# An adaLN attention block on one core: scale rows and K steps in another order, 1/sigma turned later, and a last tile in other widths

## The chip, the cores and the metric

The kernel runs on one NeuronCore of a Trainium2 chip. Its engines work side by side, each through its own list of instructions in order: TensorE (PE; its weight loads are shown apart as PEld), VectorE (DVE), ScalarE (ACT), GpSimd (POOL), and SyncE (SP), which here only issues DMA transfers. The metric is the device time of one execution in microseconds (us). The kernel before takes 99.05 us, the median of three runs (98.73 to 99.12).

## The reference

Inputs are x (2, 256, 1152), c (2, 1152), wqkv (1152, 3456), wo (1152, 1152) and w_mod (1152, 6912), all bf16. Of the six rows of modulation only shift_a, scale_a and gate_a are used.

```
mod = (silu(c) @ w_mod).reshape(B, 6, 1, D)
shift_a, scale_a, gate_a, ... = mod[:, i]
h   = layernorm(x) * (1 + scale_a) + shift_a          # eps 1e-5
qkv = h @ wqkv ; q, k, v = split(qkv)
p   = softmax(q @ k.T * D ** -0.5)                    # one head of 1152
a   = (p @ v) @ wo
return x + gate_a * a
```

## The kernel before

There are 512 tokens in four tiles of 128 (tiles 0 and 1 are batch 0, tiles 2 and 3 are batch 1), and D = 1152 is nine blocks of 128, called k here. Nearly all of the work is matmuls on PE; the order of every engine's instructions is pinned to the order in which the code emits them (`pin`, at the end), so an instruction that waits holds up all that stands behind it on its engine. A helper records the instructions, which is why the profile shows one line, L74, for almost all.

**Loads.** SP issues the loads in one queue: x tiles 1, 0 and 3; the scale rows of w_mod for the first 384 columns (wS, in five loads); K's weights of block 0 (wK, its first 1024 columns), of block 1; x tile 2; block 2; and then, by thirds of the columns, more of wS and wK, the shift rows (wH), the weights of Q and V (wqv), the gate rows (wG) and wo (wO). Eight transfers may be under way; each further issue waits for the load eight places ahead of it.

**Front.** PE runs 13 filler matmuls on a constant tile (`fillers`, junk_rhs). Meanwhile ACT and DVE form the silu of c (`silu_c`, whose last step copies it 27 times side by side into scT_rep), the token means (`dve_stats` and `dve_aggr` for tile 1, `act_mean` for the others) and the centred rows xc (`centre`). PE turns xc block by block (`turned`, into PSUM tiles tp), and DVE or ACT copies the turned blocks to xnT (`from_psum`). The variance is needed later only: `act_var`, or the statistics of DVE for tiles 1 and 3.

**Scale rows.** `scale_A(kk)` multiplies one of nine slices of wS with scT_rep, for three blocks of columns, and sums over kk into PSUM (psS0 and psSA). What comes out is 1 + scale for k = 0, 1, 2 (s1p). `scale_part` does the same for k = 3 to 5 (psM) and k = 6 to 8 (psL). DVE scales xnT by it (`scaled`), which gives hTs, the input of K without shift and without 1/sigma.

**K.** Six column blocks of K are summed in six PSUM tiles (accs), one step for each k: `k_part(k, tokens)` for k = 0 to 2 in pieces of the tokens as tiles become ready, `k_step(k)` for all 512 tokens and k = 3 to 8. Two more column blocks (`early_half`, psE) are summed for k = 0 to 2 and finished afterwards by `k_block`. K can leave out 1/sigma, because the scores are multiplied by it later (rstd_bc), and the shift, because it adds the same to all scores of a query.

**1/sigma.** POOL raises the four variances to the power of minus one half and splits each number in three bf16 parts (`rstd_parts`). `rstd_turn` turns the parts on PE (DVE copies them to parts_t), `rstd_spread` spreads them over all partitions with four matmuls (ACT copies them to rstd_bc). Nine DVE multiplications then put 1/sigma into xnT, which Q and V need.

**After K.** `shift_block` forms the shift rows (psH, sh), `modulated` the full h (hT). Q, the scores, V, the softmax and p @ v follow. DVE sums the gate rows beside them (gacc), and POOL reduces them over the partitions.

**Output.** The last loop makes the four tiles of tokens of the output in chunks of columns: nine matmuls each, then DVE multiplies by the gate and adds x. For the last 192 columns of the last tile the gate is in the weights already (wo_last) and x is added by a matmul with the identity, so a plain copy by ACT is enough (`pregated`). PSUM tiles come from three pools: six with the tag mm, and one each with the tags pa and pb; a new tile of a tag waits until the old one's readers are done.

Of the kernel before, what the change touches and what calls it, by code (L numbers as in the profile page):

```python
# [10 lines left out]
F32 = mybir.dt.float32  # L11
# [5 lines left out]
def kernel(  # L17
# [78 lines left out]
    def tok(b):  # L96
        return slice(b * N, (b + 1) * N)
# [4 lines left out]
        out=ident, in_=ident, compare_op=ALU.not_equal, fill=1.0, base=0,  # L102
        pattern=[[-1, P]], channel_multiplier=1,
    )
    junk_rhs = const.tile([P, 512], BF16)
    vec.memset(junk_rhs, 1.0)
    ones_bf = const.tile([P, P], BF16)
    gps.memset(ones_bf, 1.0)
# [36 lines left out]
    def load_k(k0, k1, c0=0, c1=D):  # L145
        spq.dma_start(out=wK[:, k0:k1, c0:c1], in_=wqkv_v[:, k0:k1, D + c0 : D + c1])
# [5 lines left out]
    load_x(3)  # L152
    for k0, k1 in PAIRS:
        load_mod(wS, 1, k0, k1, 0, CA)
    load_k(0, 1, 0, WE)
    load_k(1, 2, 0, WE)
    load_x(2)
    load_k(2, 3, 0, WE)
# [12 lines left out]


    cT = c_sb.rearrange("p b k -> p (b k)")
    junk_ps = psum.tile([P, 512], F32, tag="mm")

    def fillers(n):
        for _ in range(n):
            ten.matmul(junk_ps, lhsT=junk_rhs[:, 0:P], rhs=junk_rhs, start=True, stop=True)

    fillers(13)  # L180
    e_sb = small.tile([P, 2 * KT], F32, tag="e_sb")
# [4 lines left out]
    def silu_c():  # L186
        vec.tensor_scalar_add(out=e_sb, in0=e_sb, scalar1=1.0)
        vec.reciprocal(out=e_sb, in_=e_sb)
        vec.tensor_tensor(
            out=scT_f.rearrange("p k b -> p b k"),  # L190
            in0=c_sb,
            in1=e_sb.rearrange("p (b k) -> p b k", b=B),
            op=ALU.mult,
        )
        sca.copy(out=scT_rep, in_=scT_f.unsqueeze(2).to_broadcast([P, KT, NR // B, B]))

    def sc_rhs(kk):
# [13 lines left out]
    def dve_stats(t, s):  # L211
        vec.bn_stats(out=stats[t][:, s, :], in_=x_sb[:, t, s * CW : (s + 1) * CW])
# [8 lines left out]
    def act_mean(t):  # L221
        sca.activation(out=xc[:, t, :], in_=x_sb[:, t, :], func=ACT.Copy, accum_out=sums[:, t, 0:1])
        sca.activation(out=mv[:, t, 0:1], in_=sums[:, t, 0:1], func=ACT.Copy, scale=1.0 / D)
# [6 lines left out]
    def centre(t, c0=0, c1=D):  # L230
        vec.tensor_scalar(out=xc[:, t, c0:c1], in0=x_sb[:, t, c0:c1], scalar1=mv[:, t, 0:1], scalar2=None,
                          op0=ALU.subtract)
# [8 lines left out]
    def from_psum(eng, t, k0, k1, tp, j0=0):  # L241
        dst, srct = xnT[:, k0:k1, t * P : (t + 1) * P], tp[:, j0 : j0 + k1 - k0, :]
        if eng is vec:
            vec.tensor_copy(out=dst, in_=srct)
        else:
            sca.copy(out=dst, in_=srct)
# [41 lines left out]
    def scale_A(kk):  # L288
        for j in range(KA):
            ten.matmul(  # L290
                psS0 if j == 0 else psSA[:, j - 1, :], lhsT=wS[:, kk, j * P : (j + 1) * P], rhs=sc_rhs(kk),
                start=False, stop=(kk == KT - 1), skip_group_check=True,
            )
# [22 lines left out]
    def one(t):  # L316
        return slice(t * P, (t + 1) * P)
# [4 lines left out]
    def k_part(k, sl, first=False):  # L322
        for f in range(NACC):
            ten.matmul(
                accs[f][:, sl], lhsT=wK[:, k, f * P : (f + 1) * P], rhs=hTs[:, k, sl],
                start=first, stop=False, skip_group_check=True,
            )
# [32 lines left out]
    centre(1)  # L360
    act_mean(0)
    centre(0)
    act_mean(3)

    def bank(name="tp", n=KT - KA, pool=psum, tag="mm"):
# [4 lines left out]
    turned(tp1b, tiles_of(1, KA, KT))  # L370
    from_psum(vec, 1, 0, KA, tp1a)
    from_psum(vec, 1, KA, KT, tp1b)
    scale_A(0)
    scale_A(1)
    fillers(1)
    turned(tp0a, tiles_of(0, 0, KA))
    turned(tp0b, tiles_of(0, KA, KT))
    from_psum(vec, 0, 0, KA, tp0a)
    from_psum(sca, 0, KA, KT, tp0b)
    for kk in range(2, KT):  # L380
        scale_A(kk)
    act_var(0)

# [16 lines left out]
    for k in range(KA):  # L400
        scaled(k, one(3), s1p[:, k, 1:2])
    from_psum(sca, 3, KA, KT - 1, tp3, KA)
    k_part(2, tok(0))
    k_part(0, one(3))
    k_part(1, one(3))
    dve_stats(3, 1)
    centre(2)
    act_var(2)
    tp2 = bank(n=KT - 1, pool=psum_b, tag="pb")
    turned(tp2, tiles_of(2, 0, KT - 1))  # L410
    from_psum(vec, 2, 0, KA, tp2)
    for k in range(KA):
        scaled(k, one(2), s1p[:, k, 1:2])
    k_part(2, one(3))
    early_half(1, 0, psE)
    early_half(2, 0, psE)
    sca.copy(out=early[:, :, tok(0)], in_=psE)
    from_psum(sca, 2, KA, KT - 1, tp2, KA)
    dve_stats(3, 2)
    dve_aggr(3)  # L420
    var_eps(1)
    var_eps(3)
    rstd_parts()
    for k in range(KA - 1):
        k_part(k, one(2))
    psM = psum_a.tile([P, KA, NR], F32, tag="pa")
    for kk in range(KT):
        scale_part(psM, KA, kk)
    scaled_part(psM, KA)
    k_part(KA - 1, one(2))  # L430
    psE = psum_b.tile([P, NEARLY, N], F32, tag="pb")
    for k in range(KA):
        early_half(k, 1, psE)
# [7 lines left out]
    from_psum(vec, 3, KT - 1, KT, tp8, 0)  # L441
    from_psum(vec, 2, KT - 1, KT, tp8, 1)
    k_step(KA + 1)
    rstd_turn()
    k_step(KA + 2, 0, 1)
    rstd_spread()
    psL = psum_b.tile([P, KA, NR], F32, tag="pb")
    for kk in range(KT):
        scale_part(psL, KM, kk)
    scaled_part(psL, KM)  # L450
    k_step(KA + 2, 1, NACC)
    for k in range(KT):
        vec.tensor_tensor(out=xnT[:, k, :], in0=xnT[:, k, :], in1=rstd_bc, op=ALU.mult)
    for k in range(KM, KT):
        k_step(k)
    for f in range(NACC):
        evac(1, qkT[:, KT + f, :], accs[f])
# [154 lines left out]
        pT_sbs.append(pT)  # L612
    for gidx in range(TT * NCH):
        v_group(gidx)
    LASTW = 64
    TAILW = CW // 2
    wo_last = const.tile([P, KT, TAILW], BF16)

# [21 lines left out]
    for t in range(TT):  # L640
        b = t // NQ
        o_sb = work.tile([P, D], BF16, tag="o_sb")
        if t < TT - 1:
            chunks = [(oc * CW, CW) for oc in range(NCH)]
            dma_after = {NCH - 1: (0, D)}
        else:
            chunks = [(0, CW), (CW, CW), (2 * CW, CW - TAILW), (D - TAILW, TAILW - LASTW), (D - LASTW, LASTW)]
            dma_after = {1: (0, 2 * CW), 2: (2 * CW, CW - TAILW), 4: (D - TAILW, TAILW)}
        for ci, (c0, w_) in enumerate(chunks):
            cs = slice(c0, c0 + w_)  # L650
            last = (t == TT - 1) and (ci == len(chunks) - 1)
            pregated = (t == TT - 1) and c0 >= D - TAILW
            ps = psum.tile([P, w_], F32, tag="mm")
            if pregated:
                ten.matmul(ps, lhsT=ident, rhs=x_sb[:, t, cs], start=True, stop=False)
            for k in range(KT):
                ten.matmul(
                    ps, lhsT=attnT[:, k, t * P : (t + 1) * P],
                    rhs=(wo_last[:, k, c0 - (D - TAILW) : c0 - (D - TAILW) + w_] if pregated else wO[:, k, cs]),
                    start=(k == 0 and not pregated), stop=(k == KT - 1),  # L660
                )
            if pregated:
                sca.copy(out=o_sb[:, cs], in_=ps)
            else:
                ga = work.tile([P, CW], F32, tag="ga")
                vec.tensor_tensor(out=ga[:, :w_], in0=ps, in1=gate_bc[:, b, cs], op=ALU.mult)
                vec.tensor_tensor(out=o_sb[:, cs], in0=ga[:, :w_], in1=x_sb[:, t, cs], op=ALU.add)
            if t == NQ - 1:
                gated_columns(vec, 2 * ci, 2 * ci + 2)
            if ci in dma_after:  # L670
                d0, dw = dma_after[ci]
                dma_eng = nc.scalar if last else spq
                dma_eng.dma_start(out=out_f[t * P : (t + 1) * P, d0 : d0 + dw], in_=o_sb[:, d0 : d0 + dw])
# [36 lines left out]
```

## Time and profile before

| what | value |
|---|---|
| median of three runs | 99.05 us |
| the profiled execution | 98.6 us |
| its span, first to last instruction | 96.8 us |
| PE busy | 91.3 us (94%) |
| DVE busy | 70.7 us (73%) |
| ACT busy | 33.9 us (35%) |
| POOL busy | 22.1 us (23%) |
| moved by DMA | 21.31 MB, 220 GB/s over the span |

Rows of a timeline give the start in us from the span's first instruction, the time of one or of several instructions from first start to last end, the engine, the line, the operation, what it writes and reads, the shape, the count, and in brackets how long the engine stood idle before and what ended that. Matmuls overlap: one of 128 columns is shown with 0.22 us, though the next begins 0.056 us later, so the distance between starts is what a matmul costs. The list of waits gives the time waited in total, how many times, and the longest. A row of the stretches view gives the stretch, its length, busy time and count of each engine, then the granted clock of PE, the busy share of the DMA engines and GB/s.

### The profile page before, as it was taken

The page shows a single profiled execution, that of the slowest core. Times are in us where ns is not written, and L with a number is a line of the kernel's source. Part 1 is how long each engine was busy: PE and PEld are TensorE (multiplying, and loading weights), DVE is VectorE, ACT ScalarE, POOL GpSimd, SP SyncE. Part 2 cuts the span into 40 slices and gives each one's busy share as a digit, 9 for nine tenths or more (in the row PEclk, how much of TensorE's full clock was granted, in tenths as well). Part 3 has the DMA queues.
Part 4 walks back from the last instruction along what each step waited for, and adds up shares of the span by engine and source line. Part 5 has one row for each costly group of instructions (what it writes and reads, how often), then busy time and mean ns, then how long its engine had stood idle before and what let it go on. Part 6 is the DMA issues. An engine that isn't in the chain of part 4 may idle for free.

```text
span 96.8 us, 1825 instructions
## 1 busy us (share of the span) xinstructions
PE 91.3 (94%) x726; PEld 55.8 (58%) x731; DVE 70.7 (73%) x138; ACT 33.9 (35%) x68; POOL 22.1 (23%) x26
## 2 busy tenths in 40 slices
PE   3998989999999999999999999999999999999970
PEld 1347969554476444444448766556668765566570
DVE  2468677509985999999992999991228577998870
ACT  5189875220380972242222436332115400000010
POOL 6600005600000000000000000007999980035000
PEclk9999999999999999999999999999999999999999
DMA  2999999999999999999999501110000000303203
GB/s 80 285 340 344 321 383 374 396 388 405 402 375 403 381 413 386 375 370 365 378 401 409 218 6 43 40 26 0 0 0 0 7 0 0 122 0 122 96 31 116
DMA packets 18871, 21.31 MB, mean 220 GB/s; under 512 B 2864, under 2 KB 13360, under 8 KB 18864
## 3 DMA queue, kind: packets, MB, share of 16 engines
q1 hardware_dynamic: 18448, 21.16, 61.2%
q10 hardware_dynamic: 416, 0.05, 0.3%
q8 instruction: 5, 0.08, 0.3%
q14 instruction: 2, 0.02, 0.0%
HBM read 19.76 MB, written 1.18 MB: 216 GB/s over the span
## 4 chain that ended last, share of the span: by engine, by line
PE 91%; DVE 4%; issue 1%
PE ps L74 61%; PE acc L74 11%; PE junk_ps L74 6%; PE s_ps L74 4%; PE tp L74 2%; PE psH L74 2%; PE psE L74 1%; DVE o_sb L74 1%; DVE ga L74 1%; PE psL L74 1%; DVE hTs L74 1%; PE psM L74 1%; PE psSA L74 1%; DVE junk_rhs L74 1%; DVE stats L74 0%
## 5 line engine op out<-in xcount | busy, mean ns | idle before, releaser
L74 POOL PARTITION_ALL_REDUCE gate_bc<-gacc x2 | 13.7, 6887 | 47.0 <-DVE gacc L74 47.0
L74 DVE SCALAR_TENSOR_TENSOR gacc<-wG,scT_f,gacc 128x1152 f32<-128x1152 bf16 x16 | 22.7, 1417 | 0.5
L74 PE MATMUL ps<-wqv,hT 128*128 128x384 bf16 x108 | 17.7, 326 | 0.0
L74 PE MATMUL ps<-hT,wqv 128*128 128x512 bf16 x80 | 17.6, 379 | 0.1
L74 PE MATMUL ps<-wO,attnT 128*128 128x384 bf16 (+1 forms) x108 | 17.0, 319 | 0.0
L74 PEld LDWEIGHTS <-attnT 128*128 128x128 bf16 x126 | 11.3, 98 | 6.4
L74 PEld LDWEIGHTS <-hT 128*128 128x128 bf16 x108 | 10.6, 98 | 6.9
L74 PE MATMUL acc<-hTs,wK 128*128 128x128 bf16 (+2 forms) x88 | 13.4, 292 | 0.5 <-DVE s1p L74 0.4
L74 PEld LDWEIGHTS <-wK 128*128 128x128 bf16 x123 | 10.0, 97 | 6.5 <-DMA wK<-in_wqkv_dram 0.5
L74 PEld LDWEIGHTS <-wqv 128*128 128x128 bf16 x81 | 7.9, 98 | 9.6 <-DVE hT L74 0.4
L74 ACT CAST qkT<-ps 128x512 bf16<-128x512 f32 x10 | 5.8, 584 | 10.9 <-PE ps L74 10.9
L74 DVE TENSOR_TENSOR ga<-ps,gate_bc 128x384 f32<-128x384 f32 (+1 forms) x12 | 6.4, 537 | 2.8 <-PE ps L74 2.8
L74 ACT CAST v_sb<-ps 128x384 bf16<-128x384 f32 x10 | 4.7, 476 | 9.8 <-PE ps L74 9.8
L74 PE MATMUL junk_ps<-junk_rhs 128*128 128x512 bf16 x14 | 5.7, 580 | 1.5 <-DVE junk_rhs L74 1.5
L74 DVE TENSOR_TENSOR o_sb<-ga,x_sb 128x384 bf16<-128x384 f32 (+1 forms) x12 | 6.8, 565 | 0.4
L74 ACT CAST o_sb<-ps 128x128 bf16<-128x128 f32 (+1 forms) x2 | 0.5, 240 | 17.0 <-PE ps L74 17.0
L74 DVE TENSOR_TENSOR xnT<-xnT,rstd_bc 128x512 bf16<-128x512 bf16 x9 | 5.5, 683 | 0.0
L74 PE MATMUL ps<-hTs,wK 128*128 128x512 bf16 x19 | 4.9, 378 | 0.1
L74 DVE CAST attnT<-ps 128x512 bf16<-128x512 f32 (+1 forms) x6 | 3.5, 602 | 1.7 <-PE ps L74 1.7
L74 DVE BATCH_NORM_STATS2 stats<-x_sb 128x6 f32<-128x384 bf16 x6 | 3.2, 553 | 2.1 <-DMA x_sb<-in_x_dram 2.1
L74 PEld LDWEIGHTS <-junk_rhs 128*128 128x128 bf16 x14 | 1.9, 140 | 4.5 <-issue 3.0
L74 ACT CAST qkT<-acc 128x512 bf16<-128x512 f32 x6 | 3.0, 611 | 4.1 <-PE acc L74 4.1
(83 smaller groups left out, 91.4 us busy)
## 6 DMA issues: line engine op xcount, KB each, us to landing
wqv<-in_wqkv_dram SPq DMA_DIRECT2D x5, 864.0 KB, 10.1
wG<-in_w_mod_dram SPq DMA_DIRECT2D x3, 864.0 KB, 10.1
wO<-in_wo_dram SPq DMA_DIRECT2D x3, 864.0 KB, 8.8
wH<-in_w_mod_dram SPq DMA_DIRECT2D x4, 576.0 KB, 7.6
wS<-in_w_mod_dram SPq DMA_DIRECT2D x6, 288.0 KB, 6.4
wK<-in_wqkv_dram SPq DMA_DIRECT2D x6, 288.0 KB, 6.7
x_sb<-in_x_dram SPq DMA_DIRECT2D x4, 288.0 KB, 4.3
wqv<-in_wqkv_dram SPq DMA_DIRECT2D x3, 288.0 KB, 9.0
```

The costliest lines, as they stand in the source:

```text
L74: r = fn(*a, **k)
```

## The change

- The fillers' constant tile is 128 columns wide; the matmul reads it four times over (a repeated axis).
- K's first load, 1024 columns of block 0, is issued as two, of 384 and 640 columns.
- The copy to scT_rep is a function of its own (`silu_rep`) and stands on ACT behind the first `act_mean`.
- Four instead of two slices of the scale rows come between the turning of tile 1 and of tile 0, and the filler there is gone.
- The early columns for k = 1 and 2 of batch 0 stand around `k_part(2, tok(0))`. All of tile 3's `k_part` come before tile 2 is turned, all of tile 2's after psM. Tile 2 is centred ahead of the second statistics step of tile 3, and its variance is squared after the copy of its turned blocks.
- psL follows two of the six matmuls of k = 5; `rstd_turn` follows k = 5, and `rstd_spread` follows k = 6.
- The last tile has chunks of 384, 288, 288 and 192 columns instead of 384, 384, 192, 128 and 64. The last chunk is copied by ACT (128 columns) and DVE (64). In the program as built, that DVE copy waits for ACT's semaphore, and the last store waits for DVE's.

```diff
-    junk_rhs = const.tile([P, 512], BF16)
+    junk_rhs = const.tile([P, P], BF16)
...
-    load_k(0, 1, 0, WE)
+    load_k(0, 1, 0, CA)
+    load_k(0, 1, CA, WE)
...
-    junk_ps = psum.tile([P, 512], F32, tag="mm")
+    junk_ps = psum.tile([P, 4, P], F32, tag="mm")
...
-            ten.matmul(junk_ps, lhsT=junk_rhs[:, 0:P], rhs=junk_rhs, start=True, stop=True)
+            ten.matmul(junk_ps, lhsT=junk_rhs, rhs=junk_rhs.unsqueeze(1).to_broadcast([P, 4, P]),
+                       start=True, stop=True)
...
+
+    def silu_rep():
         sca.copy(out=scT_rep, in_=scT_f.unsqueeze(2).to_broadcast([P, KT, NR // B, B]))
...
     centre(0)
+    silu_rep()
     act_mean(3)
...
-    scale_A(0)
-    scale_A(1)
-    fillers(1)
+    for kk in range(4):
+        scale_A(kk)
     turned(tp0a, tiles_of(0, 0, KA))
...
-    for kk in range(2, KT):
+    for kk in range(4, KT):
         scale_A(kk)
...
+    early_half(1, 0, psE)
     k_part(2, tok(0))
-    k_part(0, one(3))
-    k_part(1, one(3))
+    early_half(2, 0, psE)
+    sca.copy(out=early[:, :, tok(0)], in_=psE)
+    for k in range(KA):
+        k_part(k, one(3))
+    centre(2)
     dve_stats(3, 1)
-    centre(2)
-    act_var(2)
+    dve_stats(3, 2)
     tp2 = bank(n=KT - 1, pool=psum_b, tag="pb")
     turned(tp2, tiles_of(2, 0, KT - 1))
     from_psum(vec, 2, 0, KA, tp2)
     for k in range(KA):
         scaled(k, one(2), s1p[:, k, 1:2])
-    k_part(2, one(3))
-    early_half(1, 0, psE)
-    early_half(2, 0, psE)
-    sca.copy(out=early[:, :, tok(0)], in_=psE)
+    dve_aggr(3)
     from_psum(sca, 2, KA, KT - 1, tp2, KA)
-    dve_stats(3, 2)
-    dve_aggr(3)
+    act_var(2)
     var_eps(1)
     var_eps(3)
     rstd_parts()
-    for k in range(KA - 1):
-        k_part(k, one(2))
...
     scaled_part(psM, KA)
-    k_part(KA - 1, one(2))
+    for k in range(KA):
+        k_part(k, one(2))
...
     k_step(KA + 1)
-    rstd_turn()
-    k_step(KA + 2, 0, 1)
-    rstd_spread()
+    k_step(KA + 2, 0, 2)
...
     scaled_part(psL, KM)
-    k_step(KA + 2, 1, NACC)
+    k_step(KA + 2, 2, NACC)
+    rstd_turn()
+    k_step(KM)
+    rstd_spread()
     for k in range(KT):
         vec.tensor_tensor(out=xnT[:, k, :], in0=xnT[:, k, :], in1=rstd_bc, op=ALU.mult)
-    for k in range(KM, KT):
+    for k in range(KM + 1, KT):
         k_step(k)
...
-            chunks = [(0, CW), (CW, CW), (2 * CW, CW - TAILW), (D - TAILW, TAILW - LASTW), (D - LASTW, LASTW)]
-            dma_after = {1: (0, 2 * CW), 2: (2 * CW, CW - TAILW), 4: (D - TAILW, TAILW)}
+            mid = (D - CW - TAILW) // 2
+            chunks = [(0, CW), (CW, mid), (CW + mid, mid), (D - TAILW, TAILW)]
+            dma_after = {1: (0, CW + mid), 2: (CW + mid, mid), 3: (D - TAILW, TAILW)}
...
-                sca.copy(out=o_sb[:, cs], in_=ps)
+                sca.copy(out=o_sb[:, c0 : c0 + P], in_=ps[:, 0:P])
+                vec.tensor_copy(out=o_sb[:, c0 + P : c0 + w_], in_=ps[:, P:w_])
```

1 line of the change is left out of this document (removed).

## The prediction

> **What bounds the kernel now.** I read the page first, then the chain of waits, the list of waits, the timeline engine by engine, and each load's time to landing. The page's span and the chain:
>
> ```profile
> span 96.8 us, 1825 instructions
> PE 91%; DVE 4%; issue 1%
> DVE p_f L74 <- PE s_ps L74: 1.9, 1, 1.9
> ```
>
> TensorE (PE) carries the end of the kernel almost alone. A change pays only where PE stands still, or in the tail behind its last matmul. The third line (list of waits) shows VectorE (DVE) waiting 1.9 us for the scores ahead of the softmax: gate work on DVE has room if PE gets there up to 1.9 us earlier. The matmul and output stages repeat unchanged; what PE gains before them it keeps.
>
> The front, from the timeline:
>
> ```profile
> 0.97 0.48 DVE L74 MEMSET junk_rhs<- 128x512 bf16 x1 [0.97 <-PEq L694]
> 1.51 5.30 PE L74 MATMUL junk_ps<-junk_rhs 128*128 128x512 bf16 x13 [1.51 <-DVE junk_rhs L74]
> 4.77 0.60 ACT L74 CAST scT_rep<-scT_f 128x486 bf16<-128x486 f32 x1 [0.80 <-DVE scT_f L74]
> 7.04 1.15 ACT L74 ACTIVATE xc<-x_sb 128x1152 bf16<-128x1152 bf16 x1
> 8.50 0.44 SPq L74 DMA_DIRECT2D wS<-in_w_mod_dram  x1
> 9.02 0.29 DVE L74 TENSOR_SCALAR hTs<-xnT,psS 128x256 bf16<-128x256 bf16 x1 [0.34 <-PE psSA L74]
> 9.43 0.66 PEld L74 LDWEIGHTS <-wK 128*128 128x128 bf16 x7 [0.51 <-DMA wK<-in_wqkv_dram]
> ```
>
> K's first weight load waits for its transfer until 9.43, although its data (hTs) was ready at 9.31. The row at 8.50 is the issue of the last wS load of the second column block. The window from 6.24 to 9.44 (its last columns: clock, share of the DMA engines, GB/s), and that wS load's time to landing:
>
> ```profile
> 6.24:9.44 3.20, 2.80 (x52) 2.12 (x50) 2.18 (x9) 3.14 (x8) 0.00 (x0) 1.00 1.05 351
> wS<-in_w_mod_dram SPq DMA_DIRECT2D x1, 288.0 KB, 6.0
> ```
>
> PE in the K stage (start, time, form):
>
> ```profile
> 11.46 1.69 PE L74 MATMUL acc<-hTs,wK 128*128 128x256 bf16 x18
> 13.54 0.62 PE L74 MATMUL tp<-ident,xc 128*128 128x128 bf16 x8 [0.39 <-DVE xc L74]
> 14.00 0.50 PE L74 MATMUL acc<-hTs,wK 128*128 128x128 bf16 x6
> 14.33 0.60 PE L74 MATMUL psE<-hTs,wK 128*128 128x256 bf16 x4
> 14.90 0.83 PE L74 MATMUL acc<-hTs,wK 128*128 128x128 bf16 x12
> 15.61 0.86 PE L74 MATMUL psM<-scT_rep,wS 128*128 128x54 bf16 x27
> 16.63 0.82 PE L74 MATMUL psE<-hTs,wK 128*128 128x256 bf16 x6
> 17.29 1.46 PE L74 MATMUL acc<-hTs,wK 128*128 128x512 bf16 x5
> 18.69 1.46 PE L74 MATMUL acc<-hTs,wK 128*128 128x512 bf16 x6
> 20.24 0.39 PE L74 MATMUL acc<-hTs,wK 128*128 128x512 bf16 x1
> 20.61 0.38 PE L74 MATMUL spread_ps<-parts_t,pick 12*128 12x128 bf16 x4
> 20.92 0.87 PE L74 MATMUL psL<-scT_rep,wS 128*128 128x54 bf16 x27
> ```
>
> Start to start, a matmul of 128 columns takes 0.056 us (14.00 to 14.33, six), of 256 columns 0.109 (16.63 to 17.29, six), of 512 columns 0.216 (17.29 to 18.69: six, one record missing, and two transposes), of 54 columns 0.026 (15.61: 0.86 less some 0.19 for the last, over 26). With these rates PE's holes are: 0.21 inside the 18 from 11.46; 0.55 before 13.54 (tile 2 isn't centred); 0.13 before 14.90; 0.15 before 20.61 (the spread waits for parts_t).
>
> **The change part by part.**
>
> *Front.* The memset shrinks to a quarter. Its new time lies between nothing and 0.48; I take 0.20, so the fillers start at 1.23. That hides. They now read 128 columns four times over, a form that no row shows; the columns are as many, so I take the same time; at 6.77 (6.50 for their end and some 0.27 for two small matmuls) PE begins to turn tile 1, is done at 7.27, and up to 0.03 more per filler would cost nothing. What decides is scT_rep: it now comes after ScalarE's (ACT) first mean, in the place that the second mean has in before (7.04), and is done at 7.64. PE turns tile 1, drops one filler and stands until 7.67. Then 12 scale matmuls (0.31), nine transposes (0.50), 12 more scale matmuls: the last psS starts at 8.80, takes some 0.20 and lets hTs go 0.04 later, at 9.04 against 9.02; it is done at 9.33. wK's first load in two: the first 96 of 256 KB are there 160 KB earlier, by 351 GB/s 0.46 us before 9.4, so hTs decides: first K matmul at 9.36. Minus 0.08; between minus 0.3 (memset free, ACT early) and plus 0.2 (a scT_rep delayed by DVE counts in full).
>
> ACT's queue behind scT_rep shifts by 0.50. Behind it stand mean 3, the copy of tile 0's turned columns, which the sixth accumulator's buffer waits for (9.80; needed 9.91), and the variance of tile 0. The other queues:
>
> ```profile
> 10.79 1.16 ACT L74 ACTIVATE xc<-x_sb 128x1152 bf16<-128x1152 bf16 x1 [0.33 <-DMA x_sb<-in_x_dram]
> 12.07 0.20 ACT L74 ACTIVATE mv<-sums 128x1 f32<-128x1 f32 x1
> 11.62 0.36 DVE L74 COPY xnT<-tp 128x384 bf16<-128x384 bf16 x1 [0.82 <-PE tp L74]
> 12.98 0.50 DVE L74 TENSOR_SCALAR xc<-x_sb,mv 128x1152 bf16<-128x1152 bf16 x1
> 14.20 0.36 DVE L74 COPY xnT<-tp 128x384 bf16<-128x384 bf16 x1 [0.71 <-PE tp L74]
> 15.99 0.19 POOL L74 TENSOR_SCALAR rstd<-mv 128x1 f32<-128x1 f32 x1 [0.66 <-DVE mv L74]
> 18.70 0.21 POOL L74 TENSOR_TENSOR parts<-rest,parts 128x4 bf16<-128x4 f32 x1
> ```
>
> *Reordered K steps.* The 0.33 that ACT idles at 10.79 takes most of the shift: mean 2 starts at about 10.87. tp3 ends at 11.38. Then two early columns (0.22), k_part 2 (0.65), two early columns: 12.47. Tile 3's scaled rows are ready by 12.2, so the 0.21 hole is gone. 18 matmuls of tile 3 (1.00): 13.48. Centring tile 2 no longer stands behind a statistics step: mean 2 is there by 12.4, centring runs 12.45 to 12.96, and the 0.55 hole is gone too. Transposes until 13.94. What covers these steps is that DVE's results are ready 0.3 to 0.5 us before PE asks; a later first mean or x tile 2 would bring the hole before the transposes back. Late next is psM: its last third needs the load issued at 8.50, landing at 14.5, by now perhaps 14.55 (SP has one load more to issue); it ends at 14.78. Tile 2's rows: PE's first turn to the copy is 0.66 (13.54 to 14.20), the copy to the first matmul 0.70: 13.48 plus 1.36 is 14.84. 18 matmuls (1.00), six early columns (0.66): the next full K step starts at 16.50 against 17.29, minus 0.79 with the front's share in it. The two statistics steps lie on DVE before 14.1; the variance of tile 2 is now behind the copy of its other columns on ACT (from 14.50, where DVE's copy ends, some 0.7, then 1.16 and 0.2, the rows' times for a pass and its sum) and ends at 16.5, POOL's chain (2.92 from 15.99 to the end of 18.70's, and two steps before it) at 20.0.
>
> *1/sigma two steps later.* The turn comes at 21.2, after POOL's 20.0. parts_t stands on DVE behind the six psL scalings and is done at 22.15 (psL from 19.64, its scalings from 20.75 by the same distances as in before); PE, which pays the same 0.25 for the turn as now (18.69 plus six times 0.216 to 20.24), has a whole K step (1.30) to do until 22.75: the 0.15 hole goes. PE is then 0.94 ahead. The price is on DVE:
>
> ```profile
> 21.02 0.59 ACT L74 COPY rstd_bc<-spread_ps 128x512 f32<-128x512 f32 x1 [2.95 <-PE spread_ps L74]
> 23.21 5.50 DVE L74 TENSOR_TENSOR xnT<-xnT,rstd_bc 128x512 bf16<-128x512 bf16 x9
> 29.00 0.69 DVE L74 TENSOR_TENSOR qkT<-ps,early 128x512 bf16<-128x512 f32 x1 [0.29 <-PE ps L74]
> 30.52 0.69 DVE L74 TENSOR_TENSOR qkT<-ps,early 128x512 bf16<-128x512 f32 x1 [0.83 <-PE ps L74]
> 31.43 0.18 DVE L74 COPY sh<-psH 128x18 f32<-128x18 f32 x1 [0.22 <-PE psH L74]
> ```
>
> The nine multiplies start at 23.83 (spread 22.80, plus 0.41 to the copy, 0.59 and 0.03) instead of 23.21. 1.34 us of idle time between them and sh is what they can eat: multiplies done 29.33, both additions 30.55, sh about 30.5, the moment when PE's psH is done (31.43 less 0.94). Tie: the 0.94 reaches the Q stage, with no slack left on DVE.
>
> *Tail.*
>
> ```profile
> 93.42 0.35 DVE L74 TENSOR_TENSOR ga<-ps,gate_bc 128x192 f32<-128x192 f32 x1
> 93.65 0.50 ACT L74 CAST o_sb<-ps 128x128 bf16<-128x128 f32 x2 [17.02 <-PE ps L74]
> 93.81 0.36 DVE L74 TENSOR_TENSOR o_sb<-ga,x_sb 128x192 bf16<-128x192 f32 x1
> 94.19 0.38 ACTq L673 DMA_DIRECT2D out_dram<-o_sb  x1
> ```
>
> In before, ACT copies 128 columns while PE does the last 64, then those 64. The two end at 94.15; with some 0.21 for the smaller one and 0.03 for the signal PE is done at 93.91. The chunk of 192 that takes their place has as many columns and one identity matmul less: PE ends at 93.88. ACT then copies 128 columns (the other 0.27 or so of the 0.50) from 93.92 to 94.19. In the changed program's order the new DVE copy of 64 columns waits for ACT's semaphore: the two copies run one behind the other. It lies between 0.18 (18 columns, row of 31.43) and 0.36 (384, row of 14.20); I take 0.18. The last store then starts at 94.43 against 94.19: plus 0.24, between 0.2 and 0.4. DVE's 288-wide work hides: PE is done with that chunk ten matmuls of 192 columns (0.08 each) before its end, at 93.06, and two operations of 0.46 each (between the 192-wide 0.35 and twice that) end at 94.03, ahead of 94.19. Its store starts at 94.06, earlier than the 94.19 of before, and is not the last.
>
> The Trainium skill, PSUM — Partial Sum Buffer, section on bank collisions, says that two engines must not read one bank at the same time and asks for a semaphore per bank. That agrees with the wait in the order; side by side the copies would make the sum minus 0.92 instead of minus 0.70 (98.13).
>
> *Sum:* 0.94 less 0.24 is 0.70. The profiled execution took 98.6; the new one 97.9. The median of 99.05 is 0.45 above that execution, so 98.35.
>
> **Rivals.**
> *The front gains too (97.75).* The 13 fillers take 5.30, some 0.43 each for most, twice the 0.216 of the later rows: the clock came up near their end, once, in this execution. In one where it comes after 9.4, PE bounds the front: 0.28 earlier start and a dropped filler at 0.43 are 0.7 instead of 0.08, so minus 1.3. The median's 0.45 over the profiled execution speaks for it, the one trace against. The Trainium skill, TensorE: Matmul & The Clock Gate, Part 1, says that the clock comes up with a free-running window of about 3.4 us, so its moment varies from run to run; one trace can't show it.
> *The transfers take it back (98.9).* The share 1.05 says that the engines are full, and every load behind wK issues one slot (some 0.47) later. If psM's last third lands at 15.1 instead of 14.55, K starts 0.5 later. Against it: 6.0 us from issue to landing means a deep queue.
> *Slower: the spread comes late.* The Q stage starts 6.85 after the nine multiplies (30.68 less 23.83), and each tenth that they start after 23.83 is a tenth at the end. From 25.0 on the kernel is over 0.5% slower; it takes a spread 1.2 late, by a parts_t held back behind psL's scalings or by POOL, 1.2 us from deciding. At a spread 1.5 late: 99.85.
>
> **How the numbers follow.** 0.5% (0.5 us) is about what this measurement can tell from no change. The forecast has 0.55, its own range 98.0 to 98.7; the front 0.14, the transfers 0.21, the late spread 0.10. Faster: 0.47 of the forecast's, 0.14 and 0.03, together 0.64; same 0.08 and 0.18; slower 0.10. The range reaches below to the front's case with a tenth more, 97.6, and above the transfers' case to 99.2.
>
> **What would show it.** Right: transposes of tile 2 follow tile 3's matmuls with no wait on DVE xc; six 512-column steps from about 16.5; psH about 0.95 earlier; the last store 0.24 later behind PE's last matmul. Wrong: a wait on DMA before psM above 0.3; DVE's multiplies later than 24.2; sh waiting on DVE's own additions; psS after 8.9; fillers over 0.43 each.

## The result and the profile after

The changed kernel takes 97.61 us (97.43 to 97.95), the kernel before 99.06 (98.73 to 99.12), each the median of four executions on the same chip: a ratio of 0.9865, 95% interval 0.9829 to 0.9901. A later comparison on another chip, with more executions (the first experiment), gives 0.9911 (0.9883 to 0.9940). The traces of the two pairs give 0.67 and 0.87 us between the spans. So the change is worth about 0.9 us, and the 1.45 between the first two medians is at the upper end of what was seen. Executions over 1.5% above the fastest of their kernel are left out of the medians and ratios below; u_tail's profiled execution (98.88) is one of them, but its span of 96.10 is like the others'.

The profiled execution of the changed kernel took 97.95. From its page: the span, the engines' busy time, and the shares of the chain that ended last.

```profile
span 96.2 us, 1804 instructions
PE 91.2 (95%) x715; PEld 55.5 (58%) x720; DVE 70.6 (73%) x139; ACT 33.5 (35%) x67; POOL 21.4 (22%) x26
...
PE 85%; DMA 9%; DVE 1%; SPq 1%; issue 1%; ACT 0%
```

PE has nearly the same work (91.3 us busy in before), so what the span lost is mostly PE's idle time. New in the chain is DMA, with 9%. The chain in order of time (start, time, what) says where:

```profile
1.71 4.33 DMA x_sb<-in_x_dram
...
6.05 4.32 DMA wK<-in_wqkv_dram
...
10.41 0.83 PE acc L74 x6
```

SP's issue of K's block 1 waited for x tile 3, which landed at 6.03 (1.71 plus 4.33); the block landed at 10.37, and only then could PE begin with k = 1. Block 2 landed at 11.74, by the transfers' records, and k = 2 began at 11.78. The timeline of PE through the changed stages:

```profile
1.10 5.66 PE L74 MATMUL junk_ps<-junk_rhs 128*128 128x512 bf16 x13 [1.10 <-DVE junk_rhs L74]
...
9.09 0.81 PE L74 MATMUL acc<-hTs,wK 128*128 128x256 bf16 x6 [0.33 <-DVE hTs L74]
...
10.41 0.83 PE L74 MATMUL acc<-hTs,wK 128*128 128x256 bf16 x6 [0.29 <-DMA wK<-in_wqkv_dram]
...
11.78 0.83 PE L74 MATMUL acc<-hTs,wK 128*128 128x256 bf16 x6
...
12.67 1.17 PE L74 MATMUL acc<-hTs,wK 128*128 128x128 bf16 x18
13.67 0.61 PE L74 MATMUL tp<-ident,xc 128*128 128x128 bf16 x8
14.12 0.86 PE L74 MATMUL psM<-scT_rep,wS 128*128 128x54 bf16 x27
15.02 1.17 PE L74 MATMUL acc<-hTs,wK 128*128 128x128 bf16 x18
...
16.68 1.46 PE L74 MATMUL acc<-hTs,wK 128*128 128x512 bf16 x5
...
21.46 0.22 PE L74 MATMUL turn_ps<-ident,parts 128*12 128x128 bf16 x1
...
23.02 0.39 PE L74 MATMUL spread_ps<-parts_t,pick 12*128 12x128 bf16 x4
...
25.94 1.07 PE L74 MATMUL psH<-scT_rep,wH 128*128 128x54 bf16 x36
...
32.52 3.83 PE L74 MATMUL ps<-hT,wqv 128*128 128x512 bf16 x17
```

From 11.78 to the Q stage no row has a bracket: tile 2's transposes follow tile 3's matmuls at once. By the starts one hole is left, some 0.2 before 15.02 (14.12 plus 27 times 0.026 is 14.82), while tile 2's rows are copied and scaled. Here is where the time went, by differences of such starts. "k2" is the first matmul with k = 2, "turn 2" the transposes of tile 2, "K" the first full K step, "end" PE's last matmul. The last column is from there to the moment when the last of the stores has landed, from the transfers' records.

| us | before | after | difference |
|---|---|---|---|
| start to k2 | 11.46 | 11.78 | +0.32 |
| k2 to turn 2 | 2.08 | 1.89 | -0.19 |
| turn 2 to K | 3.75 | 3.01 | -0.74 |
| K to psH | 9.30 | 9.26 | -0.04 |
| psH to Q | 6.58 | 6.58 | 0.00 |
| Q to end | 60.73 | 60.71 | -0.02 |
| end to last landing | 2.04 | 2.12 | +0.08 |

The sum is 0.59 less; the rest of the 0.67 is in how soon the program ends after the last landing. By these marks all of the gain lies between k = 2 and the first full K step. One part of it is work that passed a mark: the two early columns' matmuls for k = 1 (0.22) lie behind k2 in before and ahead of it in the changed kernel. So of the 0.93 between k2 and K some 0.7 are holes that closed, and 0.22 is work that moved ahead of k2, where PE would otherwise have stood waiting for block 2.

### The profile page after: what moved, and what is told of

The parts are those of the page before. It is cut to its first block, busy times and chain, and to the rows that moved or that the text cites. A ratio compares the mean times of both kernels' runs of the same rounds, so it can differ in the third digit from the quotient of the medians.

```text
span 96.2 us, 1804 instructions
## 1 busy us (share of the span) xinstructions
PE 91.2 (95%) x715; PEld 55.5 (58%) x720; DVE 70.6 (73%) x139; ACT 33.5 (35%) x67; POOL 21.4 (22%) x26
## 4 chain that ended last, share of the span: by engine, by line
PE 85%; DMA 9%; DVE 1%; SPq 1%; issue 1%; ACT 0%
PE ps L74 63%; PE acc L74 12%; DMA x_sb<-in_x_dram 4%; DMA wK<-in_wqkv_dram 4%; PE s_ps L74 4%; PE psH L74 2%; PE psE L74 1%; PE tp L74 1%; SPq L74 1%; PE psL L74 1%; DVE xnT L74 0%; PE spread_ps L74 0%; ACT o_sb L74 0%; DVE hTs L74 0%; DVE o_sb L74 0%
## 5 line engine op out<-in xcount | busy, mean ns | idle before, releaser
L74 PEld LDWEIGHTS <-attnT 128*128 128x128 bf16 x117 | 11.3, 98 | 6.3
L74 DVE COPY xnT<-tp 128x384 bf16<-128x384 bf16 (+2 forms) x7 | 2.2, 347 | 3.3 <-PE tp L74 3.3
L74 DVE CAST v_sb<-ps 128x384 bf16<-128x384 f32 x2 | 1.1, 558 | 4.6 <-PE ps L74 4.6
```

The source lines that it names most:

```text
L74: r = fn(*a, **k)
```

## The experiments

Except where a diff says otherwise, each is the changed kernel with one part undone. Stages are in us as in the table above; the ratio is against the kernel before on the same chip, with its 95% interval. The traces tell more than the ratios, whose intervals overlap: a stage's length repeats within some 0.01 to 0.02 from execution to execution, the start to k2 does not.

| kernel | ratio | start to k2 | k2 to turn 2 | turn 2 to K | K to psH | end to landing | span |
|---|---|---|---|---|---|---|---|
| before | | 11.46 | 2.08 | 3.75 | 9.30 | 2.04 | 96.85 |
| before2 | | 11.77 | 2.09 | 3.75 | 9.30 | 2.06 | 97.19 |
| after | 0.9865 (0.9829 to 0.9901) | 11.78 | 1.89 | 3.01 | 9.26 | 2.12 | 96.18 |
| after2 | 0.9911 (0.9883 to 0.9940) | 11.90 | 1.89 | 3.01 | 9.27 | 2.13 | 96.32 |
| u_front | 0.9891 (0.9838 to 0.9944) | 11.86 | 1.88 | 3.01 | 9.27 | 2.12 | 96.26 |
| u_mid | 0.9952 (0.9916 to 0.9988) | 11.61 | 1.92 | 3.75 | 9.26 | 2.11 | 96.78 |
| u_rstd | 0.9915 (0.9884 to 0.9947) | 12.13 | 1.89 | 3.01 | 9.64 | 2.12 | 96.91 |
| u_tail | 0.9877 (0.9818 to 0.9936) | 11.72 | 1.89 | 3.01 | 9.27 | 2.07 | 96.10 |
| u_split | 0.9929 (0.9901 to 0.9958) | 11.79 | 1.88 | 3.00 | 9.27 | 2.12 | 96.25 |
| t_act | 0.9910 (0.9882 to 0.9938) | 11.75 | 1.89 | 3.00 | 9.27 | 1.95 | 95.98 |
| t_act2 | 0.9880 (0.9831 to 0.9928) | 11.55 | 1.89 | 3.00 | 9.26 | 1.95 | 95.78 |
| e_order | | 12.40 | 2.10 | 3.11 | 9.26 | 2.12 | 97.11 |
| e_order2 | 0.9939 (0.9906 to 0.9972) | 11.27 | 2.20 | 3.11 | 9.26 | 2.12 | 96.08 |
| best | 0.9868 (0.9818 to 0.9917) | 11.76 | 2.33 | 3.01 | 9.26 | 1.95 | 96.44 |

In ten of these fourteen traces k2 begins 0.04 or 0.05 behind the landing of K's block 2 (in both of before, too). In u_front, u_split and e_order2 block 2 is there earlier, and k2 follows PE's own work; in e_order block 1 comes too late.

### The two kernels again: after2 and before2

No edit: the changed kernel and the kernel before, profiled and, the first of them, timed once more.

> The changed kernel once more, unaltered, with more rounds. Walk: it is 0.65 to 0.75 faster than before in like executions, so 98.3 against 99.0, ratio 0.993; the 1.45 of the first medians came from four executions that happened to have early first transfers. Rival: the change is worth 1.4 to 1.5, ratio 0.985, and the profiled execution of before was a fast one, of after a slow one.

> The kernel before, unaltered, for a second trace. Walk: the same holes on PE (0.2, 0.55, 0.13 and 0.15) whatever the first transfers do, Q from 33.0 to 33.5. Rival, the front: in this execution x tile 0 lands at about 4.5 as in four of the five traces since, and the first K matmul is earlier than 9.44, yet block 2's load still holds PE at 11.4 or later.

The changed kernel took 97.94 (97.67 to 98.71, 11 executions), before 98.87 (22 executions): 0.93 less. k2 lies 0.13 later in after2 than in before2 (11.90 and 11.77), where the first pair had 0.32. The stages behind it are the same to 0.02. What differs from execution to execution lies ahead of k2. One expectation failed: before2's first K matmul came at 9.76, not earlier than 9.44, since the last slice of scale rows waited 0.43 for its load; k2 is where block 2's landing (11.73) puts it all the same. In after2 PE was held there by the same kind of wait as above, one block further on:

```profile
11.90 0.83 PE L74 MATMUL acc<-hTs,wK 128*128 128x256 bf16 x6 [0.41 <-DMA wK<-in_wqkv_dram]
```

### The order of the first K steps undone: u_mid

```diff
-    early_half(1, 0, psE)
     k_part(2, tok(0))
-    early_half(2, 0, psE)
-    sca.copy(out=early[:, :, tok(0)], in_=psE)
-    for k in range(KA):
-        k_part(k, one(3))
-    centre(2)
+    k_part(0, one(3))
+    k_part(1, one(3))
     dve_stats(3, 1)
-    dve_stats(3, 2)
+    centre(2)
+    act_var(2)
...
+    k_part(2, one(3))
+    early_half(1, 0, psE)
+    early_half(2, 0, psE)
...
+    for k in range(KA - 1):
+        k_part(k, one(2))
...
-    for k in range(KA):
-        k_part(k, one(2))
+    k_part(KA - 1, one(2))
```

> The changed kernel with before's order of the first K steps (k = 0 to 2), all else as changed. Walk: the order is worth 0.71 (three holes of 0.21, 0.55 and 0.13 less a new one), so 98.3. Rival, the transfers: psM and the K steps come so early that they wait for their loads, the order is worth 0.3 to 0.4 only: 97.9 to 98.0.

It took 98.49 and the span is 96.78, 0.60 more than after's and 0.52 more than that of u_front, its neighbour on the chip. The stage from tile 2's transposes to the first full K step is back at 3.75. From PE's timeline:

```profile
11.61 1.54 PE L74 MATMUL acc<-hTs,wK 128*128 128x256 bf16 x18
13.53 0.62 PE L74 MATMUL tp<-ident,xc 128*128 128x128 bf16 x8 [0.39 <-DVE xc L74]
...
17.28 1.03 PE L74 MATMUL acc<-hTs,wK 128*128 128x512 bf16 x3
```

The wait of 0.39 for tile 2's centring is the one of before, to the hundredth. The order of the K steps is the bulk of the change: 5.67 (17.28 less 11.61) against 4.90 (16.68 less 11.78), 0.77 where the whole change is worth about 0.9. Of the 0.77, 0.22 is the early columns for k = 1, which after does ahead of k2: a gain because block 2's landing holds k2 in both (11.56 here, 11.74 in after). The other 0.55 are holes.

### 1/sigma turned and spread at its old place: u_rstd

```diff
     k_step(KA + 1)
-    k_step(KA + 2, 0, 2)
+    rstd_turn()
+    k_step(KA + 2, 0, 1)
+    rstd_spread()
...
-    k_step(KA + 2, 2, NACC)
-    rstd_turn()
-    k_step(KM)
-    rstd_spread()
+    k_step(KA + 2, 1, NACC)
```

> The changed kernel with 1/sigma turned and spread at before's place (turn after k = 4, spread one matmul later, psL after it). Walk: POOL's parts come at 19.6 in the changed kernel's trace, and the turn would stand at about 19.4 to 19.5, so PE waits 0.1 to 0.2 for POOL and 0.15 for parts_t: 97.9. Rival: the later place costs DVE's slack before the Q stage as much as it saves on PE, and it makes no difference: 97.6.

K to psH grew from 9.26 to 9.64. From its PE timeline:

```profile
20.16 0.22 PE L74 MATMUL turn_ps<-ident,parts 128*12 128x128 bf16 x1 [0.27 <-POOL parts L74]
...
26.67 1.07 PE L74 MATMUL psH<-scT_rep,wH 128*128 128x54 bf16 x36
```

PE now reaches the turn before POOL has made the parts, and stands for 0.27. In before, where K began later, the old place cost 9.30 less 9.26, 0.04. So the later place gains 0.04 by itself, and it keeps 0.38 of what the K steps' order gained. The median (98.31) stands 0.13 above that of u_front (98.18), with ratios that overlap: this verdict rests on the stage.

### The front's order undone: u_front

```diff
-    junk_rhs = const.tile([P, P], BF16)
+    junk_rhs = const.tile([P, 512], BF16)
...
     centre(0)
-    silu_rep()
     act_mean(3)
...
-    for kk in range(4):
-        scale_A(kk)
+    scale_A(0)
+    scale_A(1)
+    fillers(1)
...
-    for kk in range(4, KT):
+    for kk in range(2, KT):
```

In it the copy to scT_rep is the last step of `silu_c` again; K's first load stays in two.

> The changed kernel with before's front put back (wide constant tile, the copy to scT_rep ahead of the first mean, two slices of scale rows and a filler between the two turnings); the two loads of K's block 0 stay. Theory of the walk: the front is worth 0.08 us, so 97.7 against 97.61 of the changed kernel. Rival, the front: before's front is held up by ACT or the clock in most executions, and the 0.75 us that the sum of 0.70 leaves of the measured 1.45 lies here: 98.3 to 98.5.

```profile
9.67 0.82 PE L74 MATMUL acc<-hTs,wK 128*128 128x256 bf16 x6 [0.33 <-DVE hTs L74]
...
11.86 0.82 PE L74 MATMUL acc<-hTs,wK 128*128 128x256 bf16 x6
```

K's first matmul is 0.58 later than in after (9.09), and k2 comes at 11.86, between the 11.78 and the 11.90 of the changed kernel. The front's order moves the first matmul and hardly anything behind it: here PE works through to k2 without a wait and gets there 0.10 behind block 2 (11.76); with the earlier first matmul PE stands waiting for block 1 or 2. The median of 98.18 lies between the two forecasts, and the changed kernel was not timed on this chip. (In the nine traces that have the changed front and its loads, the first matmul came between 8.87 and 9.27, so the 9.67 is the edit's for the most part.)

### K's block 0 in one load: u_split

```diff
-    load_k(0, 1, 0, CA)
-    load_k(0, 1, CA, WE)
+    load_k(0, 1, 0, WE)
```

> The changed kernel with K's block 0 in one load of 1024 columns again. Theory: the second small load takes a place among the eight transfers under way, so block 1's load waits for x tile 3 (landing 6.03) where it waited for c; block 2 lands at 11.7 in the traces of the changed kernel against 11.4 before, and PE's step for k = 2 starts on it at 11.78. Without the split it lands 0.2 to 0.4 earlier and the whole stage moves with it: 0.2 to 0.4 us less than the changed kernel beside it. Rival, the walk: the split lets the first K matmul start 0.08 earlier and all else waits for other things: 0.0 to 0.1 us more.

After the first runs I held the second load against the change: each further issue waits for the load eight places ahead, so one load more shifts the blocks behind it. That fell. From PE's timeline:

```profile
9.59 0.83 PE L74 MATMUL acc<-hTs,wK 128*128 128x256 bf16 x6 [0.35 <-DVE s1p L74]
...
11.79 0.82 PE L74 MATMUL acc<-hTs,wK 128*128 128x256 bf16 x6
```

Block 2 did land sooner (11.59 against 11.74 and 11.85), but the first K matmul came at 9.59 against 9.09 and 9.14, so that PE itself arrived at k = 2 only at 11.79. The span is 96.25, between those of after and after2, so this trace shows the split worth nothing either way. The median is 98.22 against after2's 97.94 on the same chip, with ratios that overlap. One small thing does differ: from the last landing to the end of the span it is 0.89 here and 0.90 in both traces of before, and 0.83 or 0.84 in all eleven that have a load more; why is not shown.

### The last tile in its old widths: u_tail

```diff
+    LASTW = 64
...
-            mid = (D - CW - TAILW) // 2
-            chunks = [(0, CW), (CW, mid), (CW + mid, mid), (D - TAILW, TAILW)]
-            dma_after = {1: (0, CW + mid), 2: (CW + mid, mid), 3: (D - TAILW, TAILW)}
+            chunks = [(0, CW), (CW, CW), (2 * CW, CW - TAILW), (D - TAILW, TAILW - LASTW), (D - LASTW, LASTW)]
+            dma_after = {1: (0, 2 * CW), 2: (2 * CW, CW - TAILW), 4: (D - TAILW, TAILW)}
...
-                sca.copy(out=o_sb[:, c0 : c0 + P], in_=ps[:, 0:P])
-                vec.tensor_copy(out=o_sb[:, c0 + P : c0 + w_], in_=ps[:, P:w_])
+                sca.copy(out=o_sb[:, cs], in_=ps)
```

> The changed kernel with before's last tile (chunks of 384, 384, 192, 128, 64, ACT alone copies the last two). Walk: the two copies one behind the other cost 0.24, so 97.35 without them. Rival: the narrower middle chunks give back what the second copy costs (stores issued apart land sooner), no difference: 97.6.

First the tail of the changed kernel: its copies and the issues of the last two stores, from the timeline, then the last store (KB, us from issue to landing) from the view of the transfers.

```profile
93.27 0.27 ACT L74 CAST o_sb<-ps 128x128 bf16<-128x128 f32 x1 [17.29 <-PE ps L74]
93.42 0.33 SPq L74 DMA_DIRECT2D out_dram<-o_sb  x1
93.57 0.22 DVE L74 CAST o_sb<-ps 128x64 bf16<-128x64 f32 x1 [0.17 <-ACT o_sb L74]
93.82 0.36 ACTq L677 DMA_DIRECT2D out_dram<-o_sb  x1
```

```profile
out_dram<-o_sb ACTq DMA_DIRECT2D x1, 48.0 KB, 1.5
```

The same of u_tail, where SP's last store waits for the DVE product of the first row:

```profile
93.10 0.36 DVE L74 TENSOR_TENSOR o_sb<-ga,x_sb 128x192 bf16<-128x192 f32 x1
93.48 0.37 ACTq L676 DMA_DIRECT2D out_dram<-o_sb  x1
```

```profile
out_dram<-o_sb ACTq DMA_DIRECT2D x1, 48.0 KB, 1.8
```

In the old widths the last store is issued 0.28 behind PE's end, in the new ones 0.59, because the two copies run one behind the other. But the old one needs 1.79 to land and the new one 1.53. The old one is issued at 93.48 together with SP's last store, whose data are there at 93.46; the new one follows SP's 0.40 later. From PE's end to the last landing it is 2.07 against 2.12, and PE's end itself comes 0.02 sooner in the new widths: the new tail costs 0.03, not 0.3. The medians can't tell it: 97.94 here, where 97.35 or 97.6 was expected, against u_front's 98.18, with ratios that overlap. That the company of the other store is what slows the landing fits all the traces here: 1.76 to 1.79 when the two are issued together, 1.56 or 1.57 at 0.20 apart (t_act, below, t_act2 and best), 1.52 to 1.54 at 0.40 apart. But SP's store also differs (48 KB when issued together, 72 KB otherwise), and no run moved a store alone, so the cause stays an argument.

### ACT copies all 192 columns: t_act and t_act2

```diff
-                sca.copy(out=o_sb[:, c0 : c0 + P], in_=ps[:, 0:P])
-                vec.tensor_copy(out=o_sb[:, c0 + P : c0 + w_], in_=ps[:, P:w_])
+                sca.copy(out=o_sb[:, cs], in_=ps)
```

> The changed kernel, but ACT copies all 192 columns of the last chunk in one operation, so that VectorE's copy and its wait go. One copy of 192 columns lies between 0.27 (128 columns) and 0.35: the store starts 0.15 to 0.2 earlier, and if the store's landing is unaltered (1.53 after its start) the kernel is 0.15 to 0.2 faster than the changed kernel beside it. Rival: stores that start closer behind SP's last store land later, as in before (1.75): no difference.

> The changed kernel with ACT copying all 192 columns of the last chunk, a second time, to have it beside the kernel above: 97.7 to 97.9, ratio 0.990, from PE's last matmul to the last landing 1.95 against 2.12 of the changed kernel.

From t_act's timeline:

```profile
93.24 0.32 ACT L74 CAST o_sb<-ps 128x192 bf16<-128x192 f32 x1 [17.29 <-PE ps L74]
93.59 0.36 ACTq L676 DMA_DIRECT2D out_dram<-o_sb  x1
```

One copy of 192 columns takes 0.32; the pair takes 0.52 from the start of the first to the end of the second (93.27 to 93.79). The store is issued 0.39 behind PE's end and landing is 1.95 behind it: 0.17 less than in after, and 0.09 less than in the old tail of before (the store lands 1.56 behind its issue, little more than after's 1.53). The medians are 97.80 and 97.68, against 97.94 of after2 on t_act's chip, 0.14 less. The trace shows the gain; the intervals don't separate the two.

The same two traces speak on the clock. t_act's fillers, and its k2:

```profile
1.11 4.43 PE L74 MATMUL junk_ps<-junk_rhs 128*128 128x512 bf16 x13 [1.11 <-DVE junk_rhs L74]
...
11.75 0.50 PE L74 MATMUL acc<-hTs,wK 128*128 128x256 bf16 x3 [0.20 <-DMA wK<-in_wqkv_dram]
```

The same 13 fillers took 4.43 here and 5.66 in after: the full clock was granted at 4.08 here and at 6.57 there, by the clock's own records (3.8 to 6.9 over the thirteen traces that have one). k2 came at 11.75 and 11.78, 0.05 and 0.04 behind block 2 in both: here the moment of the clock does not reach k2.

### Block 2 loaded before x tile 2: e_order and e_order2

```diff
-    load_x(2)
     load_k(2, 3, 0, WE)
+    load_x(2)
```

> The changed kernel with x tile 2 loaded behind K's block 2 instead of ahead of it. Theory of the transfers: PE's step for k = 2 starts when block 2's load has landed (11.46 and 11.77 before, 11.78 and 11.90 changed); 288 KB less ahead of it, at 350 to 370 GB/s some 0.75, and it starts at 11.1 to 11.3. Tile 2 is then centred 0.7 later, and PE waits for that before it turns tile 2 (at 13.9 to 14.1 against 13.7). Rival, the walk: k = 2 starts at 11.6 to 11.9 as before, because PE, ACT and DVE set it and not the load.

> The changed kernel with x tile 2 loaded behind K's block 2, a second time, since in the first look K's block 1 landed at 11.03, 0.7 to 2 us later than in any other trace, and hid what the order does. If that was one execution's transfers: k = 1 starts at 10.0 to 10.4, k = 2 at 11.1 to 11.3, tile 2's turning waits for its centring until 13.9 to 14.1, the time is 0.1 to 0.4 over the changed kernel's 97.94. If the order itself does it: block 1 lands at 11 again, k = 2 starts after 12.2, and the time is near 99.0.

e_order tells little: in its execution block 1 landed at 11.03, already late. The order alone doesn't do that: in e_order2, with the same loads, it landed at 9.38.

```profile
11.07 0.83 PE L74 MATMUL acc<-hTs,wK 128*128 128x256 bf16 x6 [0.87 <-DMA wK<-in_wqkv_dram]
```

e_order2, the same kernel, had block 2 landed at 10.16. Its PE timeline, and a line from its list of waits (total, count, longest):

```profile
11.27 0.82 PE L74 MATMUL acc<-hTs,wK 128*128 128x256 bf16 x6
...
13.46 0.61 PE L74 MATMUL tp<-ident,xc 128*128 128x128 bf16 x8 [0.16 <-ACT xnT L74]
```

```profile
PE tp L74 <- DVE xc L74: 1.3, 1, 1.3
```

With the weights there, k2 comes at 11.27 with no wait on a transfer: 0.5 to 0.6 before after's and after2's. So K's loads hold k2 in the changed kernel: in after block 1's, from 10.41 on, and block 2's, which landed just as PE got there (11.74), so that either would have held it; in after2 block 2's. But x tile 2 is now late, tile 2 is centred late, and its transposes begin at 13.46, 0.2 to 0.3 before those two instead of 0.5. The median is 98.18, no better than the changed kernel.

### Less to load before k = 2: best

t_act with the early columns' weights (64 KB of each of the blocks 0 to 2) loaded behind block 2, and their matmuls placed behind k = 2:

```diff
-    load_k(0, 1, 0, CA)
-    load_k(0, 1, CA, WE)
-    load_k(1, 2, 0, WE)
+    CB = NACC * P
+    load_k(0, 1, 0, CB)
+    load_k(1, 2, 0, CB)
     load_x(2)
-    load_k(2, 3, 0, WE)
+    load_k(2, 3, 0, CB)
+    load_k(0, KA, CB, WE)
...
-    early_half(0, 0, psE)
...
-    early_half(1, 0, psE)
     k_part(2, tok(0))
-    early_half(2, 0, psE)
+    for k in range(KA):
+        early_half(k, 0, psE)
```

> The changed kernel with ACT copying all 192 columns of the last chunk, and with the two early columns of K's blocks 0 to 2 (64 KB each) loaded behind block 2, their matmuls all behind k_part 2. Theory of the transfers: 192 KB less ahead of block 2's load, some 0.5; k = 2 starts at 11.2 to 11.4, tile 2 is turned at 13.5 to 13.6 against 13.7 to 13.8, so 0.15 to 0.25 less than with ACT's copy alone, 0.3 to 0.4 less than the changed kernel. Rival: tile 2's centring or the later small load holds PE instead, and nothing is gained over ACT's copy alone.

It took 97.51 (97.32 to 98.31), t_act2 beside it 97.68 (97.07 to 98.17), before 98.79. The profiled execution was the slowest of the six:

```profile
11.76 0.83 PE L74 MATMUL acc<-hTs,wK 128*128 128x256 bf16 x6 [0.49 <-DMA wK<-in_wqkv_dram]
```

PE stands ready for k = 2 at about 11.3, earlier than in after, and waits for block 2 all the same, which landed at 11.72; k = 2 had been expected at 11.2 to 11.4. Whether the other executions, which were 0.16 to 0.99 shorter, got their weights sooner wasn't seen. It isn't shown to beat t_act2: 0.17 between medians whose executions spread over 1 us.

What stays open is why the first transfers end at such different times: among these fourteen traces tile 0 of x landed between 4.38 and 5.62, without any order by the kernel's edit, and k2 began between 11.27 and 12.40.

## Why the prediction came out as it did

The time of 97.61 lies at the lower edge of the range (97.6), with the forecast at 98.35. That the range holds it is luck: its lower end was drawn for the rival "The front gains too", whose mechanism fell. On the later chip 97.94 stands 0.93 under before, where 0.70 was forecast. By steps:

**Front, "minus 0.08": the step stopped too early.** The first K matmul was forecast at 9.36 and came at 9.09 and 9.14: the load in two was in time, as said, and PE didn't have to stand until 7.67 for scT_rep, which ACT began at 5.88 instead of 7.04. But the step ended there. Behind it the working let k = 2 follow PE's own work, at 11.60, 0.14 later than in before because two early columns now lie ahead of it. It came at 11.78 and 11.90, because the working passed over when block 1 and block 2 of K land, which SP issues one slot later: 10.37 and 11.74 in after, 11.85 for block 2 in after2. From start to k2 the changed kernel is later by 0.32 in one pair and by 0.13 in the other; how much of that is the change and how much the execution's transfers isn't shown. In both of before's traces, too, k2 begins 0.04 or 0.05 behind block 2's landing (11.41 and 11.73), and PE gets there no sooner: a tie, which the transfers' times showed ahead of the result and the working left out.

**Reordered K steps: right in mechanism and in size.** From k2 to the first full K step the working gives 11.60 to 16.50, 4.90; the traces of the changed kernel have 4.90 (16.68 less 11.78) and 4.89, where before has 5.83. In both the two early columns are moved ahead of k2. The holes of 0.55, 0.21 and 0.13 are gone, the 0.2 before tile 2's matmuls is as the working had it, tile 2's transposes follow without a wait on xc, and u_mid, with the old order, has the 0.39 wait again. One piece fell: psM was to wait for its last load until 14.55. It ran from 14.12 to 14.98 without a wait, and the path went where the working had it, through DVE's copy and tile 2's scaling; from the transposes to tile 2's matmuls it is 1.35 (13.67 to 15.02) against 1.36 forecast.

**1/sigma two steps later: the gain mis-sized, the price right.** The "0.15 hole" before the spread was to go, and 0.04 went. The chain in order of time shows why. First before, then after2, where parts_t was there long before:

```profile
20.30 0.32 PE acc L74
20.63 0.36 PE spread_ps L74 x4
20.99 0.80 PE psL L74 x27
```

```profile
20.09 0.70 PE psL L74 x27
...
21.80 1.40 PE acc L74 x6
23.20 0.32 PE spread_ps L74 x4
23.52 2.70 PE acc L74 x12
```

In before one matmul ahead of the spread takes 0.32, 0.10 over its 0.216; in after2, where parts_t was done at 22.40, six take 1.40, 0.10 over six times 0.216. Behind the spread it is alike: psL takes 0.80 there and 0.70 elsewhere, and the twelve matmuls 2.70, 0.11 over theirs. So PE pays some 0.1 on the way into the spread and 0.1 on the way out, at either place, and most of what I read as a wait for parts_t was that price. In before parts_t was there 0.06 ahead of the spread (20.55 and 20.61):

```profile
20.34 0.21 DVE L74 COPY parts_t<-turn_ps 12x128 bf16<-12x128 bf16 x1 [1.09 <-PE turn_ps L74]
```

By the starts the hole went from 0.15 to 0.10 (21.73 plus six times 0.216 to 23.13 in after2), so the wait can't have cost more than some 0.05. The move was needed all the same, for a reason the step didn't give: at the old place PE would now wait for POOL, 0.38 in u_rstd. The tie on DVE came out as forecast. From after's timeline of DVE:

```profile
22.09 0.20 DVE L74 COPY parts_t<-turn_ps 12x128 bf16<-12x128 bf16 x1
24.06 5.51 DVE L74 TENSOR_TENSOR xnT<-xnT,rstd_bc 128x512 bf16<-128x512 bf16 x9 [1.77 <-ACT rstd_bc L74]
29.49 1.28 DVE L74 TENSOR_TENSOR qkT<-ps,early 128x512 bf16<-128x512 f32 x2
30.78 0.18 DVE L74 COPY sh<-psH 128x18 f32<-128x18 f32 x1
```

parts_t is done at 22.29, 0.7 ahead of the spread. The multiplies start 1.04 behind the spread (1.03 forecast), and the additions and sh follow them without a gap. sh starts 4.84 after psH both here (30.78 less 25.94) and in before (31.43 less 26.59), so the additions took nothing from PE. (They end 1.20 behind the multiplies; the 1.22 of the working is not the sum of its two rows of 0.69, which are shorter one behind the other.) And psH to Q is 6.58 in all traces.

**Tail, "plus 0.24": 0.03 to 0.06.** The serial copies are there, with DVE's at 0.22 where 0.18 was taken, and the last store stands 0.59 behind PE's end. The Trainium skill, PSUM — Partial Sum Buffer, on bank collisions, gave the reason for that wait; the rows agree in the order (93.27 plus 0.27, then 93.57), and no run let the two copies overlap. The step failed by stopping at the store's issue: the landing was taken as unchanged, and it is 0.23 to 0.26 shorter. From the start of the Q stage to the last landing it is 62.83 and 62.84 in the changed kernel, 62.77 and 62.80 in before, 62.80 in u_tail.

**From the execution to the median, "0.45 above".** I carried the 0.45 between before's profiled execution (98.6) and its median over to the changed kernel. There the profiled execution (97.95) is the slowest of four, 0.34 above the median. That one term is the difference between forecast and result: for the execution 97.9 was forecast and 97.95 came. That this fits so well is luck in part. On the second pair the executions (98.20 and 99.09) differ by 0.89, where the steps give 0.70: the tail is 0.20 better than the working and the K steps 0.02, 1/sigma 0.12 worse; 0.06 is the program's end behind the last landing, which no step had, and 0.02 lies outside the span.

**The rivals.** "The front gains too" was nearest to the time, but its mechanism fell: the clock came up between 3.8 and 6.9, and k2 doesn't follow it, since loads hold it. The Trainium skill, TensorE: Matmul & The Clock Gate, Part 1, says that this moment varies with the phase of a free-running window, by 500 ns either way; the traces agree that it varies, but over 3.1 us. "The transfers take it back" had the right engine and the wrong place: weights of K ahead of k = 2, not psM's load. "The spread comes late" didn't happen: POOL's last part begins at 19.55 and takes 0.20, forecast done at 20.0. (Its 6.85 is the way from the multiplies to the end of sh, 6.90 in after; the Q stage begins 8.46 behind them.)

## What to carry to other kernels

Follow a step until the next thing that every path must pass: here the first K matmul moved by half a microsecond and the third step did not follow, because it also needs a load that lands no sooner. The same holds at the end: a store that starts 0.3 later behind PE's end landed 0.05 to 0.08 later. A hole in front of an instruction is a wait only if it goes when the awaited thing comes early.

## What the runs showed of the hardware

- A last store of 48 KB landed 1.52 to 1.57 us after its issue when issued 0.4 or 0.2 behind another queue's store, and 1.76 to 1.79 when the two were issued together.
- On the way into the four spread matmuls, whose weights have 12 rows, PE loses 0.10 us, and as much on the way out, although in after2 nothing that they need is late.
- ACT copies 192 columns from PSUM in 0.32 and 128 columns in 0.27; DVE takes 0.22 for 64. Splitting so small a copy between two engines that must take turns costs 0.2 (0.52 against 0.32).
- The moment of the full clock varied by 3.1 us between executions (3.8 to 6.9), and the landing of x tile 0 by 1.2 (4.38 to 5.62). Neither says when k2 begins: it follows the landing of K's block 2 by 0.04 or 0.05 in ten of fourteen traces, and that landing lies between 11.5 and 12.1 in the eight traces that have the changed kernel's loads in their order. What moves it wasn't found.
